# Attention scores as one product per key block, three exponentials per head pair, and tail columns copied by VectorE

## The chip, the cores and the metric

The kernel runs on one core of a Trainium2 chip. The metric is the device time of a run in microseconds; lower is better. The kernel before took 343.55 us in the median of three runs (343.11 to 345.07).

## What is computed

Causal attention with a decay ("forgetting attention"), and behind it a two-layer network with SiLU. There are 8 batches, 8 heads, 576 positions of 64 values; the network is 512 to 2048 to 512 wide over 4608 tokens.

```python
scores = scale * np.matmul(q, k.transpose(0, 1, 3, 2))
cum = np.cumsum(np.log(np.clip(f, 0.0001, 1.0)), axis=-1)
decay = cum[:, :, :, None] - cum[:, :, None, :]
scores = np.where(causal, -1000000000.0, scores + decay)
attn = softmax(scores)                    # written out in the reference
x = np.matmul(attn, v)                    # heads side by side: 4608 x 512
h = x @ w_in
out = (h * (1.0 / (1.0 + np.exp(-h)))) @ w_out
```

The decay is folded into the values: row j of v, and a column of ones beside it, is multiplied by exp(-cum[j]) up to a factor that the division by the sum takes out again. So the kernel needs the exponential of the plain scores, a 0/1 mask on the diagonal blocks, one product with the weighted values, and a division by the product's last column.

## The kernel before

**Stages.** The first 128 queries of all batches (they see only key block 0) are done early. The other 448 queries of a head, "the rest", are done in 32 units, one for each batch and pair of heads (`scores`, `attend`), and the network's two products (`m1_chunk`, L567, and `m2_part`, L612) are dealt out between them. From about 281 us on only the network's products are left.

**Order.** The order of every engine's instructions is the order in which the program issues them (`manual_schedule`), so each engine works through a queue written out by hand. The loop at L874 runs 16 times; I call one pass a round, and its two units n and n+1. A round has three slots of network work (L886, L892, L898) with score products in front of each: chunks 0 and 1 of n; chunk 2 of n and chunk 0 of n+1; chunks 1 and 2 of n+1. Behind the third slot come `attend(n)` and `attend(n+1)`, then a fourth slot. `fill` decides by a count of matmul columns how many network products a slot gets; it knows nothing of the other engines.

**A unit's scores.** A product takes a key block of 128 keys (its 64 values a head on 64 of the 128 rows of TensorE; the pair's second head uses the other 64) and some query columns. `CHUNKS` (L433) gives three PSUM tiles `sc` of two banks a unit, of which two exist: (key block, first column, last column, place). Columns 0 to 384 are queries 128 to 512, columns 384 to 448 the last 64 queries, "the tail". Before, the tail of each of the five key blocks is a product of its own of 64 columns in chunk 2. That makes 12 products a head and unit, 24 a unit.

**Exponentials and masks.** ScalarE takes the exponential of chunks 0 and 1 with 2 x 512 columns each (L463), of chunk 2 with 2 x 128 columns (L463) and, apart from it, of the tails with 2 x 5 x 64 columns (L467). The first three go into the unit's SBUF tile `u` (four buffers), the last into `ut`, one of four tiles with a strip of zeros between the two heads. VectorE multiplies the three diagonal blocks by the 0/1 triangle `tri` in one instruction (`mask`, L476) and the last 64 keys of the tail by `trit` (`mask_tail`, L482).

**Attend.** `attend` forms 28 products with the weighted values into a PSUM tile `dn` (L506 for the rest, L515 for the tail), then VectorE divides (L523, L524). `AT` says where in `u` a block lies.

**The network.** `m1_chunk` writes a PSUM tile `hp` (L567); ScalarE takes a tanh of it (`th`, L575) and VectorE forms `gt` from both (L576). `hp`, `po`, `dn` and `tx` share four PSUM buffers (tag "big"): a product into a fifth tile waits until an earlier one has been read. The last reader of `hp` is L576.

**The feed.** SP's queue loads q, k and v of later units (L158, L168, L179), GpSimd casts q and k to bf16 (L399, L403, three instructions a unit), SP transposes them by DMA into `qkT` (L427, two units ahead), and GpSimd weights the values (`convert_v`, L413, four instructions a batch, in the third and fourth unit of the batch before). From round 3 on SP also transposes the finished rows of the round before (L538, L542).

Of the kernel before, what the change touches and what calls it, by code (L numbers as in the profile page):

```python
# [8 lines left out]
ACT = mybir.ActivationFunctionType  # L9
ALU = mybir.AluOpType  # L10
FP32 = mybir.dt.float32
BF16 = mybir.dt.bfloat16
P = 128
# [5 lines left out]
def kernel(  # L19
# [10 lines left out]
    nc = tc.nc  # L30
# [7 lines left out]
    SM = 512  # L38
    ST = S - SM
    NM = SM // P  # L40
    NR = NM - 1
    RB = NR * P
    RQ = RB + ST
# [8 lines left out]
    scale = 1.0 / float(D) ** 0.5  # L52
# [24 lines left out]
    tri = const.tile([P, P], BF16, name="tri")  # L77
    trit = const.tile([P, ST], BF16, name="trit")
# [6 lines left out]
    uts = [const.tile([P, NM + 1, 3, ST], BF16, name=f"ut_{i}") for i in range(4)]  # L85
# [63 lines left out]
    def head(p, i):  # L149
        return p // 2 * 4 + 2 * i + p % 2  # L150
# [69 lines left out]
    for i in range(2):  # L220
        for g in range(2):
            nc.vector.tensor_copy(
                out=sel[:, i, :].rearrange("p (u w r) -> p u w r", u=2, w=2)[:, g, :, :],
                in_=ident_bf[:, :].rearrange("p (r u i w) -> p u i w r", u=2, i=2, w=2)[
                    :, g, i, :, :
                ],
            )

    def keep_warm(n):
# [7 lines left out]
        out=f_sb[:, :], in0=f_sb[:, :], scalar1=1e-4, scalar2=1.0, op0=ALU.max, op1=ALU.min  # L237
# [185 lines left out]
    def transposes(n):  # L423
# [5 lines left out]
        )  # L429


    T0 = P
    CHUNKS = [  # L433
        [(1, 0, P, 0), (2, P, 2 * P, P), (3, 2 * P, RB, 2 * P), (1, P, 2 * P, RB)],
        [(0, 0, RB, 0), (1, 2 * P, RB, RB)],
        [(2, 2 * P, RB, 0)] + [(kb, RB, RQ, T0 + kb * ST) for kb in range(NM + 1)],
    ]
    UW = 2 * SM + P

    AT = {(c, c): (c - 1) * P for c in range(1, NM)}  # L440
    AT |= {(c, 0): SM + (c - 1) * P for c in range(1, NM)}
    AT |= {(2, 1): RB, (3, 1): SM + RB, (3, 2): 2 * SM}

    def scores(n, c):
        b, p = divmod(n, NP)
        if c == 0:
            us[n] = upool.tile([P, 2, UW], BF16, name="u", tag="u")
        u, ut = us[n], uts[n % 4]
        t = qkT[n]
        sc = psc.tile([P, 2, SM], FP32, name="sc", tag="sc")  # L450
        for kb, q0, q1, o in CHUNKS[c]:
            for i in range(2):
                r = slice(i * D, (i + 1) * D)
                if kb == 0:
                    kt = kT0[b][r, p, :]
                else:
                    k0 = RB if kb == NM else kb * P + RB
                    kt = t[r, k0 : k0 + P]
                nc.tensor.matmul(  # L459
                    sc[:, i, o : o + q1 - q0], lhsT=kt, rhs=t[r, q0:q1], start=True, stop=True  # L460
                )
        w = SM if c < 2 else T0
        nc.scalar.activation(  # L463
            out=u[:, :, c * SM : c * SM + w], in_=sc[:, :, 0:w], func=ACT.Exp, scale=scale
        )
        if c == 2:
            nc.scalar.activation(  # L467
                out=ut[:, :, 0:3:2, :].rearrange("p k i t -> p i k t"),
                in_=sc[:, :, T0 : T0 + (NM + 1) * ST].rearrange("p i (k t) -> p i k t", t=ST),
                func=ACT.Exp,  # L470
                scale=scale,
            )

    def mask(n):
        x = us[n][:, :, 0:RB].rearrange("p i (a t) -> p i a t", t=P)
        nc.vector.tensor_tensor(  # L476
            out=x, in0=x, in1=tri[:, None, None, :].to_broadcast([P, 2, NR, P]), op=ALU.mult
        )

    def mask_tail(n):  # L480
        x = uts[n % 4][:, NM, 0:3:2, :]
        nc.vector.tensor_tensor(  # L482
            out=x, in0=x, in1=trit[:, None, :].to_broadcast([P, 2, ST]), op=ALU.mult
        )

    NGR = 2 * NR + 1
# [3 lines left out]
    def attend(n):  # L490
        b, p = divmod(n, NP)
        if p % 2 == 0:
            xqs[n // 2] = xqp.tile([P, NGR, 2, D], BF16, name="xr", tag="xr", bufs=3)
        xq = xqs[n // 2]
        u, ut = us.pop(n), uts[n % 4]
        dn = pbig.tile([P, NGR, D + 1], FP32, name="dn", tag="big")

        def vals(kb, i):
            h = head(p, i)
            return v0[b][:, h, :] if kb == 0 else vbf[b][:, kb - 1, h, :]  # L500

        for i in range(2):
            for c in range(1, NM):
                for kb in range(c + 1):
                    o = AT[c, kb]
                    nc.tensor.matmul(  # L506
                        dn[:, i * NR + c - 1, :],
                        lhsT=u[:, i, o : o + P],
                        rhs=vals(kb, i),
                        start=(kb == 0),  # L510
                        stop=(kb == c),
                    )
        for i in range(2):
            for kb in range(NM + 1):
                nc.tensor.matmul(  # L515
                    dn[:, NGR - 1, :],
                    lhsT=ut[:, kb, i : i + 2, :].rearrange("p i t -> p (i t)"),
                    rhs=vals(kb, i),
                    start=(i == 0 and kb == 0),
                    stop=(i == 1 and kb == NM),  # L520
                )
        rec = recp.tile([P, NGR], FP32, name="rec", tag="rec")
        nc.vector.reciprocal(out=rec[:, :], in_=dn[:, :, D])  # L523
        nc.vector.tensor_tensor(  # L524
            out=xq[:, :, p % 2, :],
            in0=dn[:, :, 0:D],
            in1=rec[:, :, None].to_broadcast([P, NGR, D]),
            op=ALU.mult,
        )
# [58 lines left out]
    def store(n):  # L588
        n = max(n, 0)
        for q_, dst, src in stores[:n]:  # L590
            q_.dma_start(out=dst, in_=src)  # L591
        del stores[:n]
# [105 lines left out]
    def fill(us_, least=0, ends=(0, 0)):  # L698

        left = us_ + at["left"]  # L700
        kinds = plan(left)
        kinds += [0] * (least - len(kinds))
        if any(ends) and kinds:
            if 2 not in kinds:
                kinds[0] = 2
            n1, n2 = len(kinds) - kinds.count(2), kinds.count(2)
            e0 = 1 if ends[0] else 0
            e1 = 1 if ends[1] and n2 > e0 else 0
            inner = n2 - e0 - e1
            n = n1 + inner  # L710
            mid = [2 if (x + 1) * inner // n > x * inner // n else 1 for x in range(n)]
            if inner and mid[-1] == 2 and e1 and not e0:
                mid = mid[::-1]
            kinds = [2] * e0 + mid + [2] * e1
        for k in kinds:
            t = step(k)
            if t is None:
                at["left"] = 0.0
                return
            left -= t / 1000  # L720
        at["left"] = left
# [117 lines left out]
    def turn(n):  # L839
        if 0 < n < NU - 2:  # L840
            cast_qk(n + 2)
            transposes(n + 2)

    def prepare(n):

        b, p = divmod(n, NP)
        if n != NP - 1 and n + 4 < NU:
            load_qk(n + 4)
        if b + 1 == B:
            return  # L850
        if p == 0 and b > 0:
            load_tails(b + 1)
        if b == 0 and p >= 2 or b > 0 and p == 1:
            for c in range(NM) if b > 0 else range(2 * (p - 2), 2 * (p - 1)):
                load_v(b + 1, c)
        if n == NP - 1:
            load_qk(n + 4)
        if p >= 2:
            for c in range(2 * (p - 2), 2 * (p - 1)) if b > 0 else range(NM * (p - 2)):
                convert_v(b + 1, c)  # L860
# [4 lines left out]
    def slot(us_, *ends):  # L865
        n = len(stores)
        fill(us_, 0, ends)
        store(n)
        for x in pending:
            x[0] -= 1  # L870
        while pending and pending[0][0] == 0:
            ready.update(pending.pop(0)[1])

    for m in range(NQ):  # L874
        n = 2 * m
        piece = 1.7 if m < 2 else 2.4
        scores(n, 0)
        scores(n, 1)
        turn(n)
        if m > 0:  # L880
            back(m - 1)
            if m % 2 == 0:
                b = m // 2 - 1
                pending.append([2, [REST_OF[b]] + ([TAILS_OF[b][0]] if b == NM - 1 else [])])
        prepare(n)
        slot(piece, 1, 0)  # L886
        mask(n)
        scores(n, 2)
        scores(n + 1, 0)
        turn(n + 1)  # L890
        prepare(n + 1)
        slot(piece, 1, 0)  # L892
        mask_tail(n)
        mask(n + 1)
        scores(n + 1, 1)
        scores(n + 1, 2)
        mask_tail(n + 1)
        slot(piece, 1, 0)  # L898
        attend(n)
        attend(n + 1)  # L900
        slot(min(3.5, max(0.8, behind() - LAG)) if m > 1 else 0.8)
# [38 lines left out]
```

## Time and profile before

| | before |
|---|---|
| median of three runs | 343.55 us |
| span of the profiled execution, first to last instruction | 342.2 us |
| median less span | 1.35 us |
| TensorE busy, matmuls | 334.3 us, 3560 matmuls |
| VectorE busy | 180.5 us, 387 instructions |
| ScalarE busy | 216.8 us, 401 instructions |
| GpSimd busy | 130.0 us, 227 instructions |
| score matmuls of the rest, L459 | 768 |
| granted TensorE clock | 0.999 |

The profiled execution has no time of its own besides its span; what lies around the span is taken as the difference to the median.

The page gives for each engine (PE is TensorE, DVE VectorE, ACT ScalarE, POOL GpSimd, SPq the queue of SP) busy time, share and number of instructions. A line of the groups view has line, engine, operation, output tile <- input tiles, shapes, count, then busy time and mean duration in ns, then the idle time of the engine in front of it and what ended that. A line of the timeline has start, duration, engine, line, operation, tiles, count; in brackets the idle time before it and its releaser. Matmuls are pipelined, so a matmul's duration is its latency, and what it costs is read from the starts.

### The profile page before, as it was taken

Reading aid. Unit: us, or ns where it says so; the run is one execution under the profiler, and the core shown is the slowest. Engines: PE = TensorE matmul, PEld = TensorE weight load, DVE = VectorE, ACT = ScalarE, POOL = GpSimd, SP = SyncE. Lnnn points to the kernel's source line nnn. Section 1 sums busy time; section 2 is a strip of 40 time slices with the busy share of each in tenths; the row PEclk is TensorE's granted clock in tenths of the full one; section 3 lists DMA queues with packets and bytes.
Section 4 is the critical chain, followed back from the end, with each engine's and each line's share of the span. In section 5 each row is a group of like instructions: output and inputs, shape, how many; then the busy total and the mean of one; then the engine's idle time right before and its main releaser. Section 6 shows DMA issues by size and latency. Waiting matters only on the chain.

```text
span 342.2 us, 8881 instructions
## 1 busy us (share of the span) xinstructions
PE 334.3 (98%) x3560; PEld 198.6 (58%) x3560; DVE 180.5 (53%) x387; ACT 216.8 (63%) x401; POOL 130.0 (38%) x227
## 2 busy tenths in 40 slices
PE   7999999999999999999999999999999999999995
PEld 3645655567656556566465666656656565555654
DVE  4665736357647547357445563655746364444330
ACT  5857645877687676857759677595685944454431
POOL 8895317732618307327325422612830000001011
PEclk9999999999999999999999999999999999999999
DMA  8999999999699889999999789989994010001012
GB/s 154 185 184 221 192 192 155 233 207 190 142 172 205 188 177 168 180 210 156 174 188 188 171 156 202 169 170 165 165 186 101 22 42 33 31 32 61 33 53 72
DMA packets 142457, 50.67 MB, mean 148 GB/s; under 512 B 133328, under 2 KB 139728, under 8 KB 142416
## 3 DMA queue, kind: packets, MB, share of 16 engines
q1 hardware_dynamic: 132400, 32.93, 56.7%
q0 software_dynamic: 9856, 17.04, 21.5%
q8 instruction: 28, 0.46, 0.6%
q10 hardware_dynamic: 160, 0.13, 0.1%
q14 instruction: 13, 0.11, 0.1%
HBM read 36.85 MB, written 9.44 MB: 135 GB/s over the span
## 4 chain that ended last, share of the span: by engine, by line
PE 66%; DMA 14%; SPq 9%; POOL 6%; issue 3%; ACT 0%; POOLq 0%
PE po L612 29%; PE hp L567 25%; DMA vf<-in_v_dram 6%; PE sc L459 5%; SPq L158 5%; PE dn L506 4%; DMA w_out_bf<-in_moe_w_out_dram 3%; PE dn L515 2%; SPq L427 2%; DMA qkT<-qkb 2%; POOL qkb L399 1%; DMA qkb<-in_k_dram 1%; SPq L168 1%; SPq L179 1%; DMA qf<-in_q_dram 1%
## 5 line engine op out<-in xcount | busy, mean ns | idle before, releaser
L576 DVE SCALAR_TENSOR_TENSOR gt<-th,hp 128x384 bf16<-128x384 bf16 (+2 forms) x208 | 105.8, 522 | 119.0 <-ACT th L575 115.5
L575 ACT ACTIVATE th<-hp 128x384 bf16<-128x384 f32 (+2 forms) x208 | 95.2, 478 | 84.3 <-PE hp L567 82.0
L612 PE MATMUL po<-w_out_bf,gt 128*128 128x512 bf16 (+1 forms) x592 | 145.3, 374 | 0.0
L567 PE MATMUL hp<-x,w_in_bf 128*128 128x384 bf16 (+2 forms) x704 | 128.1, 321 | 0.2
L567 PEld LDWEIGHTS <-w_in_bf 128*128 128x128 bf16 x832 | 79.9, 98 | 56.5 <-issue 0.7
L463 ACT ACTIVATE u<-sc 128x1024 bf16<-128x1024 f32 (+1 forms) x96 | 75.3, 822 | 9.5 <-PE sc L459 9.5
L612 PEld LDWEIGHTS <-gt 128*128 128x128 bf16 x592 | 53.3, 98 | 47.9 <-issue 2.5
L591 POOL DMA_DIRECT2D out_dram<-osb x38 | 21.0, 552 | 93.7 <-ACT osb L622 66.7
L413 POOL TENSOR_TENSOR vp<-vf,w_bf 128x520 bf16<-128x520 f32 (+1 forms) x32 | 34.4, 1078 | 41.0 <-DMA vf<-in_v_dram 35.1
L622 ACT ACTIVATE osb<-po 128x512 f32<-128x512 f32 (+1 forms) x37 | 22.1, 597 | 18.9 <-PE po L612 18.9
L399 POOL CAST qkb<-qf 128x384 bf16<-128x384 f32 x32 | 16.7, 521 | 41.9 <-DMA qf<-in_q_dram 41.2
L459 PE MATMUL sc<-qkT 64*128 64x128 bf16 (+1 forms) x640 | 26.9, 207 | 0.9 <-DMA qkT<-qkb 0.8
L459 PEld LDWEIGHTS <-qkT 64*128 64x128 bf16 x640 | 18.4, 94 | 12.5 <-issue 10.2
L467 ACT ACTIVATE ut<-sc 128x640 bf16<-128x640 f32 x32 | 23.3, 729 | 0.0
L476 DVE TENSOR_TENSOR u<-u,tri 128x768 bf16<-128x768 bf16 x32 | 22.1, 690 | 1.2 <-ACT u L463 1.2
L399 POOL CAST qkb<-kf 128x384 bf16<-128x384 f32 x32 | 17.7, 554 | 13.0 <-DMA kf<-in_k_dram 12.8
L506 PEld LDWEIGHTS <-u 128*128 128x128 bf16 x576 | 20.8, 98 | 2.5
L506 PE MATMUL dn<-vp,u 128*128 128x65 bf16 x384 | 21.8, 194 | 0.0
L524 DVE TENSOR_TENSOR xr<-dn,rec 128x448 bf16<-128x448 f32 x32 | 20.0, 624 | 1.1
L506 PE MATMUL dn<-v,u 128*128 128x65 bf16 x192 | 19.8, 194 | 0.0
L482 DVE TENSOR_TENSOR ut<-ut,trit 128x128 bf16<-128x128 bf16 x32 | 11.2, 351 | 15.6 <-ACT ut L467 15.6
L567 PE MATMUL hp<-xt,w_in_bf 128*128 128x256 bf16 x128 | 17.7, 273 | 0.0
(68 smaller groups left out, 203.0 us busy)
## 6 DMA issues: line engine op xcount, KB each, us to landing
out_dram<-osb POOLq DMA_DIRECT2D x32, 256.0 KB, 3.3
vf<-in_v_dram SPq DMA_DIRECT2D x26, 256.0 KB, 4.7
qf<-in_q_dram SPq DMA_DIRECT2D x64, 96.0 KB, 2.9
kf<-in_k_dram SPq DMA_DIRECT2D x64, 96.0 KB, 3.1
w_in_bf<-in_moe_w_in_dram POOLq DMA_DIRECT2D x4, 512.0 KB, 6.9
w_out_bf<-in_moe_w_out_dram POOLq DMA_DIRECT2D x4, 512.0 KB, 9.6
vf<-in_v_dram POOLq DMA_DIRECT2D x6, 256.0 KB, 10.3
qkb<-in_q_dram POOLq DMA_DIRECT2D x8, 128.0 KB, 5.1
```

Source lines behind the costliest of these rows:

```text
L399: nc.gpsimd.tensor_copy(out=t2[:, c0 : c0 + NR, :].rearrange("p c x -> p (c x)"), in_=t[:, :, :, :].rearrange("p c h d -> p (c h d)"),)
L413: nc.gpsimd.tensor_tensor(out=vbf[b][r, c, :, :], in0=vst[b][c][r, :, :], in1=w_bf[r, c + 1, b * H : (b + 1) * H, None].to_broadcast([n, H ...
L459: nc.tensor.matmul(sc[:, i, o : o + q1 - q0], lhsT=kt, rhs=t[r, q0:q1], start=True, stop=True)
L463: nc.scalar.activation(out=u[:, :, c * SM : c * SM + w], in_=sc[:, :, 0:w], func=ACT.Exp, scale=scale)
L467: nc.scalar.activation(out=ut[:, :, 0:3:2, :].rearrange("p k i t -> p i k t"), in_=sc[:, :, T0 : T0 + (NM + 1) * ST].rearrange("p i (k t) ...
L476: nc.vector.tensor_tensor(out=x, in0=x, in1=tri[:, None, None, :].to_broadcast([P, 2, NR, P]), op=ALU.mult)
L506: nc.tensor.matmul(dn[:, i * NR + c - 1, :], lhsT=u[:, i, o : o + P], rhs=vals(kb, i), start=(kb == 0), stop=(kb == c),)
L567: nc.tensor.matmul(hp[:, :], lhsT=w_in_bf[:, cc, fc * P : (fc + 1) * P], rhs=xcols(g, cc), start=(cc == 0), stop=(cc == NCC - 1),)
L575: nc.scalar.activation(out=th[:, :], in_=hp[:, :], func=ACT.Tanh, scale=0.5)
L576: nc.vector.scalar_tensor_tensor(out=gt[:, fc, :], in0=th[:, :], scalar=1.0, in1=hp[:, :], op0=ALU.add, op1=ALU.mult,)
L612: nc.tensor.matmul(po[:, :], lhsT=gt[:, fc, tb * P : (tb + 1) * P], rhs=w_out_bf[:, fc, m0:m1], start=(fc == 0), stop=(fc == NFC - 1),)
L622: nc.scalar.activation(out=osb[:, :], in_=po[:, :], func=ACT.Copy, scale=0.5)
```

## The change

The tail is no longer a product of its own: the last 64 queries are columns of the same product as the others. A unit has 5 products a head instead of 12 (two for key blocks 2 and 3 in chunk 0, block 1 and the last 64 keys in chunk 1, block 0 in chunk 2), and the columns are the same, 1472 a head. Each chunk has one exponential, into `u`, which becomes wider (1472 columns a head, 1152 before). Since `attend` wants the tail in `ut`, VectorE now copies it there: the last 64 keys with the mask in one instruction (`mask_tail`, from `u` to `ut`), the other four blocks with two copies a unit (`tails`). The mask of the diagonal blocks becomes two instructions, one for blocks 2 and 3 and one for block 1. In `ut` the strips change places (`UT`). The queues of GpSimd and SP keep their order, and so does TensorE's, the score products apart.

```diff
     CHUNKS = [
-        [(1, 0, P, 0), (2, P, 2 * P, P), (3, 2 * P, RB, 2 * P), (1, P, 2 * P, RB)],
-        [(0, 0, RB, 0), (1, 2 * P, RB, RB)],
-        [(2, 2 * P, RB, 0)] + [(kb, RB, RQ, T0 + kb * ST) for kb in range(NM + 1)],
+        [(2, P, RQ, 0), (3, 2 * P, RQ, RQ - P)],
+        [(1, 0, RQ, 0), (NM, RB, RQ, RQ)],
+        [(0, 0, RQ, 0)],
     ]
...
-        w = SM if c < 2 else T0
+        w = SM if c < 2 else RQ
         nc.scalar.activation(
             out=u[:, :, c * SM : c * SM + w], in_=sc[:, :, 0:w], func=ACT.Exp, scale=scale
         )
-        if c == 2:
-            nc.scalar.activation(
-                out=ut[:, :, 0:3:2, :].rearrange("p k i t -> p i k t"),
-                in_=sc[:, :, T0 : T0 + (NM + 1) * ST].rearrange("p i (k t) -> p i k t", t=ST),
-                func=ACT.Exp,
-                scale=scale,
-            )
...
+    def mask(n, kbs):
+        u = us[n]
+        if len(kbs) == 2:
+            o, step_ = UO[2], UO[3] - UO[2]
+            x = u[:, :, o : o + 2 * step_].rearrange("p i (a t) -> p i a t", t=step_)[:, :, :, 0:P]
+            m_ = tri[:, None, None, :].to_broadcast([P, 2, 2, P])
+        else:
+            x = u[:, :, UO[1] : UO[1] + P]
+            m_ = tri[:, None, :].to_broadcast([P, 2, P])
+        nc.vector.tensor_tensor(out=x, in0=x, in1=m_, op=ALU.mult)
...
     def mask_tail(n):
         nc.vector.tensor_tensor(
-            out=x, in0=x, in1=trit[:, None, :].to_broadcast([P, 2, ST]), op=ALU.mult
+            out=uts[n % 4][:, UT[NM], 0:3:2, :],
+            in0=us[n][:, :, UO[NM] : UO[NM] + ST],
+            in1=trit[:, None, :].to_broadcast([P, 2, ST]),
+            op=ALU.mult,
         )
+
+    def tails(n, kbs):
+        o0, o1 = (UO[kb] + RB - UQ[kb] for kb in kbs)
+        u = us[n]
+        e = o1 - o0
+        a0 = o0 - (e - ST)
+        x = u[:, :, a0 : a0 + 2 * e].rearrange("p i (k t) -> p i k t", t=e)[:, :, :, e - ST : e]
+        x0 = UT[kbs[0]]
+        nc.vector.tensor_copy(
+            out=uts[n % 4][:, x0 : x0 + 2, 0:3:2, :].rearrange("p k i t -> p i k t"), in_=x
+        )
...
         slot(piece, 1, 0)
-        mask(n)
+        mask(n, (2, 3))
+        mask(n, (1,))
+        mask_tail(n)
+        tails(n, (2, 3))
         scores(n, 2)
         scores(n + 1, 0)
         turn(n + 1)
         prepare(n + 1)
         slot(piece, 1, 0)
-        mask_tail(n)
-        mask(n + 1)
+        tails(n, (1, 0))
+        mask(n + 1, (2, 3))
+        tails(n + 1, (2, 3))
         scores(n + 1, 1)
         scores(n + 1, 2)
+        mask(n + 1, (1,))
         mask_tail(n + 1)
+        tails(n + 1, (1, 0))
         slot(piece, 1, 0)
         attend(n)
         attend(n + 1)
```

## The prediction

> **What bounds the kernel now.** I read the table of engines first, then the matmul groups by shape, then the timeline of one round.
>
> ```profile
> PE 334.3 (98%) x3560; PEld 198.6 (58%) x3560; DVE 180.5 (53%) x387; ACT 216.8 (63%) x401; POOL 130.0 (38%) x227
> ```
>
> TensorE has work in flight for 98% of the span. From 111.8 to 280 us it is busy 168.20 of 168.20 us at full clock, so only two things can move the end: matmul time itself, or a new wait of TensorE. In the stage of the rounds the waits view has just two waits of score matmuls, both on the transposed queries (0.4 us at 74.38 and at 111.78). The rows that the change touches, by shape:
>
> ```profile
> L463 ACT ACTIVATE u<-sc 128x1024 bf16<-128x1024 f32 x64 | 64.5, 1035 | 9.5 <-PE sc L459 9.5
> ...
> L467 ACT ACTIVATE ut<-sc 128x640 bf16<-128x640 f32 x32 | 23.3, 729 | 0.0
> L476 DVE TENSOR_TENSOR u<-u,tri 128x768 bf16<-128x768 bf16 x32 | 22.1, 690 | 1.2 <-ACT u L463 1.2
> ...
> L463 ACT ACTIVATE u<-sc 128x256 bf16<-128x256 f32 x32 | 12.7, 396 | 0.0
> L482 DVE TENSOR_TENSOR ut<-ut,trit 128x128 bf16<-128x128 bf16 x32 | 11.2, 351 | 15.6 <-ACT ut L467 15.6
> ```
>
> **TensorE.** Per unit 12 pairs of score matmuls become 5; the columns stay 1472 a head. Here is one group (start, duration, engine, line):
>
> ```profile
> 153.82 0.23 PE L459 MATMUL sc<-qkT 64*128 64x128 bf16 x2
> 153.89 0.19 PE L459 MATMUL sc<-qkT,kT 64*128 64x64 bf16 x2
> 153.92 0.50 PE L459 MATMUL sc<-qkT 64*128 64x64 bf16 x16
> 154.35 0.39 PE L612 MATMUL po<-w_out_bf,gt 128*128 128x512 bf16 x1
> ```
>
> Durations are latencies; starts tell the cost. The two heads of a pair start 3 ns apart and run side by side. A pair of 64 columns costs 29 ns from start to start (64 columns at 2.4 a ns are 26.7), a pair of 128 columns 56 (53.3), one of 384 columns 162 to 175 (160). So a removed pair is worth 2.5 ns and wide ones may cost some of it back: 7 x 2.5 = 17 ns a unit, 0.56 us over 32 units, between 0.1 and 0.7. Going into a group of 64-row matmuls and out of it costs about 98 and 95 ns, whatever the width beside it (64, 128, 384 columns); the 48 groups stay. What is saved before 111.78 goes into the wait there. I take **-0.4 us**.
>
> **ScalarE.** 396 and 729 ns become one instruction of 896 elements: 396 + 640 x (1035 - 396)/768 = 929 ns, 196 ns less a unit, 6.3 us in all. ScalarE is 63% busy and TensorE hardly waits for it (0.28 and 0.18 us near 63 and 66 us, ahead of the wait at 74.38, which swallows them). In a round the third slot's first tanh can come up to 0.4 us earlier, which gives VectorE some room; I count that below.
>
> **VectorE.** Two instructions a unit become five. Undisturbed, L476 takes 0.55 us for 768 elements and L482 0.22 us for 128, so 0.15 us + 0.52 ns an element. The two new masks are 0.42 and 0.28, the tail mask 0.22. A copy of 256 elements between SBUF tiles has no row: 0.22 at least (four elements a cycle; L257, 512 elements, took 0.29) and 0.28 at two a cycle. Together 1.36 us against 0.77, 19 us more over 32 units on an engine that is idle 162 us, mostly waiting for a tanh. By busy time this is hidden. But SBUF-to-SBUF work of VectorE is held by work of GpSimd, and that decides. In the round near 244 us, VectorE and then GpSimd:
>
> ```profile
> 243.81 1.12 DVE L482 TENSOR_TENSOR ut<-ut,trit 128x128 bf16<-128x128 bf16 x1
> 244.85 0.55 DVE L476 TENSOR_TENSOR u<-u,tri 128x768 bf16<-128x768 bf16 x1
> 245.32 1.07 DVE L482 TENSOR_TENSOR ut<-ut,trit 128x128 bf16<-128x128 bf16 x1
> 246.32 0.54 DVE L576 SCALAR_TENSOR_TENSOR gt<-th,hp 128x384 bf16<-128x384 bf16 x1
> ```
>
> ```profile
> 243.80 2.51 POOL L413 TENSOR_TENSOR vp<-vf,w_bf 128x520 bf16<-128x520 f32 x2
> ```
>
> L482 needs 0.22 us and takes 1.12 and 1.07: each time it ends as an L413 (1.05 us) ends. The second L413 in turn waits for L476. They take turns, one for one; L576, which reads PSUM, is never stretched (0.54 to 0.56 us in all 128). So during a run of casts and conversions each held VectorE instruction costs a whole GpSimd instruction. Now the round near 158 us, VectorE and GpSimd:
>
> ```profile
> 157.11 1.02 DVE L576 SCALAR_TENSOR_TENSOR gt<-th,hp 128x384 bf16<-128x384 bf16 x2 [1.64 <-ACT th L575]
> 158.05 0.22 DVE L482 TENSOR_TENSOR ut<-ut,trit 128x128 bf16<-128x128 bf16 x1
> 158.18 0.86 DVE L476 TENSOR_TENSOR u<-u,tri 128x768 bf16<-128x768 bf16 x1
> 159.29 0.23 DVE L482 TENSOR_TENSOR ut<-ut,trit 128x128 bf16<-128x128 bf16 x1 [0.24 <-ACT ut L467]
> 159.67 1.02 DVE L576 SCALAR_TENSOR_TENSOR gt<-th,hp 128x384 bf16<-128x384 bf16 x2 [0.16 <-ACT th L575]
> ```
>
> ```profile
> 155.96 2.15 POOL L413 TENSOR_TENSOR vp<-vf,w_bf 128x520 bf16<-128x520 f32 x2 [4.95 <-DMA vf<-in_v_dram]
> 158.05 0.58 POOL L399 CAST qkb<-qf 128x384 bf16<-128x384 f32 x1
> 158.58 0.83 POOL L399 CAST qkb<-kf 128x384 bf16<-128x384 f32 x1
> 159.36 0.31 POOL L403 CAST qkb<-qktf 128x128 bf16<-128x128 f32 x1
> 159.63 2.18 POOL L413 TENSOR_TENSOR vp<-vf,w_bf 128x520 bf16<-128x520 f32 x2
> ```
>
> Queued behind the masks is the third slot's first gt (159.67 to 160.22). It frees the PSUM buffer that the second unit's dn takes: TensorE starts that dn at 160.28, 0.06 us later. Any delay of this gt is a stall of TensorE.
>
> After the change six instructions stand there: copy, mask of two blocks, copy, mask of one, tail mask, copy. If all six take turns: copy after the L413 that ends at 158.11; cast to 158.68; mask (streams 0.27) to 158.95; cast to 159.45; copy to 159.52; small cast to 159.81; mask to 159.94; L413 to 160.99; tail mask to 161.06; L413 to 162.11; copy to 162.2; gt at 162.3 instead of 159.67. TensorE waits 2.55 us. The same count gives these waits, after the room each gt has now (0.05 to 0.42 us): near 130 us 2.3; 158 us 2.55; 186 us 1.4; 214 us 1.25; 244 us 0.3; 88 us 0.15; 104 us 0.55. Sum 8.5. Done on the present order, the count puts the gt 0 to 0.4 us later than traced; less that, 7.1. The one at 104 us (0.25 left) disappears in the wait at 111.78: 6.85. In the other rounds no run of conversions stands beside these masks, or the gt has over 0.7 us of room. Less 0.6 for the earlier tanh and exponentials: **+6.2 us**. The first mask group of a round (four instructions for one) lies under two exponentials, 2 us of ScalarE: nothing.
>
> Whether the copies take turns is not shown. For it: L730, a copy of 64 elements at 7.88 us, took 0.47 and ended with a GpSimd DMA issue (8.33). Against: L257 ran 0.29 us beside another issue, unstretched. The ends are 0 (copies free: then three held instructions stand in the third group, as now) and 8.5; nearest is L482, the same bytes in the same place, which is held. I take held.
>
> The Trainium skill (page "SBUF — State Buffer", section "Who interferes with whom") says that a Vector copy in a two-port mode and a GpSimd instruction exclude each other for a whole instruction. By that rule the sum is the held one; without it, the free one.
>
> GpSimd loses turns too, at most 0.27 us each, three more a unit, in front of casts that feed transposes; their tiles are issued 2.7 to 12 us ahead of use. Counted at zero up to 1 us.
>
> **Sum.** Span 342.2 - 0.4 + 6.2 = 348.0. The median of the runs shown, 343.55, is 1.35 above the span, so 349.4.
>
> **Rivals.**
> 1. *The copies are not held* (ends not slower). Place: the same third group. Three held instructions as now; the gt is then at 159.7 to 160.1, a stall of 0 to 0.4 us in two or three rounds, +0.6, against -0.4 and -0.6: 343.2. It decides as soon as a copy beside an L413 or a cast lasts under 0.3 us. For: L257; TensorE has no other new wait. Against: L482's rows. Chance 0.28.
> 2. *The runs move apart.* Waits of TensorE shift the loads behind SP's transposes of the last round, so casts fall between the groups and half of the waits go: 346.5. Part of the held case's spread.
> 3. *Fewer, wider matmuls give more than 2.5 ns a pair*, 98 ns at a group's edge included. At most one edge a group, 48 x 0.097 = 4.7 us: 339. Against: the edges don't depend on width. Chance 0.06.
> 4. *Held, and the feed falls behind as well*: 354. Chance 0.06.
>
> Held as forecast, from 345.5 to 353: 0.60. The range goes from the free copies to the held ones with room: 342.6 to 353. About 0.5% (1.7 us) is what a measurement of this kernel can tell from no change: faster 0.07, same 0.30, slower 0.63.
>
> **What would show it.** Steps right: score matmuls 320, L463 96 with one form of 896 elements near 0.93 us; copies stretched to 0.5 to 1.1 us beside casts and L413; first dn of the second unit late by 1 to 2.5 us near 130, 158, 186, 214 us; TensorE idle or waiting on DVE gt. Wrong: copies of 0.2 to 0.3 us everywhere; no new wait of TensorE; ScalarE's saving showing in the end.

## The result and the profile after

The change makes the kernel a little slower: 346.23 us (345.31 to 348.19) against 344.52 us (343.11 to 346.17) in 13 runs each, a ratio of 1.0055 (95% interval 1.0033 to 1.0077). The profiled execution took 345.31 us with a span of 343.5 us, 1.3 us over the span of before.

Line numbers are now those of after: L476 and L479 are the masks, L493 is the copy, L517 and L526 are the products of `attend` for the rest and the tail, L578 is `m1_chunk`, L587 the `gt`, L623 `m2_part`. The table of engines and one line of the waits view of after:

```profile
PE 335.1 (98%) x3112; PEld 191.5 (56%) x3112; DVE 197.3 (57%) x483; ACT 215.5 (63%) x369; POOL 128.5 (37%) x227
```

```profile
PE dn L517 <- DVE gt L587: 1.7, 2, 1.0
```

TensorE has 448 matmuls less, VectorE 96 instructions and 16.8 us more, and TensorE waits for a `gt` in front of a `dn`, for which the waits view of before has no line. The groups by shape that stand for the ones shown of before:

```profile
L463 ACT ACTIVATE u<-sc 128x896 bf16<-128x896 f32 x32 | 29.7, 929 | 0.0
...
L493 DVE COPY ut<-u 128x256 bf16<-128x256 bf16 x64 | 21.3, 337 | 3.5 <-ACT u L463 3.5
...
L476 DVE TENSOR_TENSOR u<-u,tri 128x512 bf16<-128x512 bf16 x32 | 16.5, 517 | 0.3
...
L476 DVE TENSOR_TENSOR u<-u,tri 128x256 bf16<-128x256 bf16 x32 | 12.0, 374 | 5.2 <-ACT u L463 5.2
...
L479 DVE TENSOR_TENSOR ut<-u,trit 128x128 bf16<-128x128 bf16 x32 | 8.0, 249 | 0.0
```

The merged exponential takes 929 ns. The copy's mean of 337 ns hides two kinds: 42 of the 64 take 0.21 to 0.23 us, ten 0.24 to 0.35, twelve 0.49 to 1.10.

The round near 133 us of after, first VectorE, then GpSimd, then TensorE:

```profile
130.29 0.57 DVE L493 COPY ut<-u 128x256 bf16<-128x256 bf16 x1
130.78 0.72 DVE L476 TENSOR_TENSOR u<-u,tri 128x512 bf16<-128x512 bf16 x1
131.42 0.31 DVE L493 COPY ut<-u 128x256 bf16<-128x256 bf16 x1
131.65 1.17 DVE L476 TENSOR_TENSOR u<-u,tri 128x256 bf16<-128x256 bf16 x1
132.74 0.21 DVE L479 TENSOR_TENSOR ut<-u,trit 128x128 bf16<-128x128 bf16 x1
132.87 1.07 DVE L493 COPY ut<-u 128x256 bf16<-128x256 bf16 x1
133.87 0.54 DVE L587 SCALAR_TENSOR_TENSOR gt<-th,hp 128x384 bf16<-128x384 bf16 x1
```

```profile
130.27 0.50 POOL L399 CAST qkb<-qf 128x384 bf16<-128x384 f32 x1
130.72 0.51 POOL L399 CAST qkb<-kf 128x384 bf16<-128x384 f32 x1
131.17 0.48 POOL L403 CAST qkb<-qktf 128x128 bf16<-128x128 f32 x1
131.62 2.24 POOL L413 TENSOR_TENSOR vp<-vf,w_bf 128x520 bf16<-128x520 f32 x2
```

```profile
133.18 0.28 PE L526 MATMUL dn<-vp,ut 128*128 128x65 bf16 x4
134.46 0.19 PE L517 MATMUL dn<-v,u 128*128 128x65 bf16 x1 [0.99 <-DVE gt L587]
```

This is the forecast's mechanism to the letter. The mask of 0.28 us and the copy of 0.22 us take 1.17 and 1.07, each as long as one of the two L413 beside it (the two end near 132.7 and 133.86); the first `gt` of the third slot can start only at 133.87, and the second unit's `dn`, whose buffer it frees, starts at 134.46. The four matmuls before it follow each other at 0.03 us, so it would have started at 133.30.

Measured from start to start like that, the waits for `gt` are 0.88 us (107.58), 1.16 us (134.46) and 0.25 us (161.80), 2.29 in all, and there is none in the eight rounds behind. (The waits view counts less, because it starts at the modelled end of the matmul before.) Against it stand the shorter products. The start of the rounds, after less before: -0.36 us in round 1, 0.00 in round 2, +1.45 in round 6, 1.52 in round 8, 1.28 in the last: from round 8 on after gains 0.034 us a round.

### The profile page after: what moved, and what is told of

It reads as the page before. It is cut to its first block, busy times and chain, and to the rows that moved or that the text cites. A ratio compares the mean times of both kernels' runs of the same rounds, so it can differ in the third digit from the quotient of the medians.

```text
span 343.5 us, 8049 instructions
## 1 busy us (share of the span) xinstructions
PE 335.1 (98%) x3112; PEld 191.5 (56%) x3112; DVE 197.3 (57%) x483; ACT 215.5 (63%) x369; POOL 128.5 (37%) x227
## 4 chain that ended last, share of the span: by engine, by line
PE 86%; DVE 5%; ACT 3%; DMA 2%; issue 1%; POOL 1%
PE po L623 35%; PE hp L578 32%; PE sc L459 6%; PE dn L517 4%; PE tp L285 2%; PE dn L526 2%; DMA qkT<-qkb 2%; DVE gt L587 2%; DVE ut L493 2%; PE wm L232 1%; ACT u L463 1%; ACT th L586 1%; PE sc L300 1%; DVE u L476 1%; PE sc L319 1%
## 5 line engine op out<-in xcount | busy, mean ns | idle before, releaser
L587 DVE SCALAR_TENSOR_TENSOR gt<-th,hp 128x384 bf16<-128x384 bf16 (+2 forms) x208 | 105.6, 522 | 110.0 <-ACT th L586 106.6
L623 PE MATMUL po<-w_out_bf,gt 128*128 128x512 bf16 (+1 forms) x592 | 145.2, 374 | 0.0
L578 PE MATMUL hp<-x,w_in_bf 128*128 128x384 bf16 (+2 forms) x704 | 128.2, 321 | 0.2
L578 PEld LDWEIGHTS <-w_in_bf 128*128 128x128 bf16 x832 | 79.9, 98 | 56.5 <-issue 0.9
L463 ACT ACTIVATE u<-sc 128x1024 bf16<-128x1024 f32 (+1 forms) x96 | 90.1, 997 | 9.5 <-PE sc L459 9.5
L623 PEld LDWEIGHTS <-gt 128*128 128x128 bf16 x592 | 53.3, 98 | 52.2 <-issue 9.3
L413 POOL TENSOR_TENSOR vp<-vf,w_bf 128x520 bf16<-128x520 f32 (+1 forms) x32 | 33.8, 1059 | 36.2 <-DMA vf<-in_v_dram 34.5
L476 DVE TENSOR_TENSOR u<-u,tri 128x512 bf16<-128x512 bf16 x64 | 27.2, 445 | 5.5 <-ACT u L463 5.2
L517 PEld LDWEIGHTS <-u 128*128 128x128 bf16 x576 | 20.9, 97 | 4.6 <-issue 2.1
L493 DVE COPY ut<-u 128x256 bf16<-128x256 bf16 x64 | 21.3, 337 | 3.5 <-ACT u L463 3.5
L459 PE MATMUL sc<-qkT 64*128 64x320 bf16 (+3 forms) x256 | 22.2, 272 | 0.9 <-DMA qkT<-qkb 0.8
L517 PE MATMUL dn<-vp,u 128*128 128x65 bf16 x384 | 21.8, 193 | 0.0
L517 PE MATMUL dn<-v,u 128*128 128x65 bf16 x192 | 19.8, 193 | 1.8 <-DVE gt L587 1.7
L578 PE MATMUL hp<-xt,w_in_bf 128*128 128x256 bf16 x128 | 17.7, 273 | 0.0
L459 PEld LDWEIGHTS <-qkT 64*128 64x128 bf16 x256 | 9.5, 94 | 14.3 <-issue 10.6
L526 PE MATMUL dn<-vp,ut 128*128 128x65 bf16 x256 | 14.1, 194 | 0.0
```

Of the source, the lines that this page charges most:

```text
L413: nc.gpsimd.tensor_tensor(out=vbf[b][r, c, :, :], in0=vst[b][c][r, :, :], in1=w_bf[r, c + 1, b * H : (b + 1) * H, None].to_broadcast([n, H ...
L459: nc.tensor.matmul(sc[:, i, o : o + q1 - q0], lhsT=kt, rhs=t[r, q0:q1], start=True, stop=True)
L463: nc.scalar.activation(out=u[:, :, c * SM : c * SM + w], in_=sc[:, :, 0:w], func=ACT.Exp, scale=scale)
L476: nc.vector.tensor_tensor(out=x, in0=x, in1=m_, op=ALU.mult)
L493: nc.vector.tensor_copy(out=uts[n % 4][:, x0 : x0 + 2, 0:3:2, :].rearrange("p k i t -> p i k t"), in_=x)
L517: nc.tensor.matmul(dn[:, i * NR + c - 1, :], lhsT=u[:, i, o : o + P], rhs=vals(kb, i), start=(kb == 0), stop=(kb == c),)
```

## The experiments

All ratios are to before, on the same chip; in brackets the 95% interval. In the expectations H is the forecast's mechanism (the copies are held by GpSimd, the `gt` comes late, TensorE waits), F a rival (the feed: GpSimd loses turns and delivers the transposed queries late), W another (VectorE's added work and its place in the queue, held or not). P and A came up with the first results, and are explained at e5.

**e1: copies through one port.** The copies become a maximum over an axis of length 1, same data, same place.

```diff
-        nc.vector.tensor_copy(
-            out=uts[n % 4][:, x0 : x0 + 2, 0:3:2, :].rearrange("p k i t -> p i k t"), in_=x
+        nc.vector.tensor_reduce(
+            out=uts[n % 4][:, x0 : x0 + 2, 0:3:2, :].rearrange("p k i t -> p i k t"),
+            in_=x[:, :, :, :, None],
+            op=ALU.max,
+            axis=mybir.AxisListType.X,
         )
```

> The changed kernel, its 64 tail copies done by VectorE as a reduction over an axis of length one in place of a copy; same place, same data, same number. Theory H (copies held by GpSimd): this form is not held, so no instruction on L493 lasts over 0.5 us, though each takes longer alone (0.35 to 0.45 us for 0.22); the waits of TensorE at the second unit's dn (0.88, 1.16 and 0.25 us in the profile after) are gone but for 0.3 us; ratio to before 0.997 to 1.001. Rival W (it is VectorE's added work and its place in the queue, held or not): the waits stay or grow, ratio 1.005 or more. Rival F (the feed: GpSimd, held by VectorE, casts later, and the transposed queries come later): between, with the wait at 73 us (1.06 us) as it is.

Measured 344.56 us, ratio 1.000 [0.9977, 1.0023]. The same round, VectorE and GpSimd of e1 (L590 is the `gt` here):

```profile
130.74 0.41 DVE L493 TENSOR_REDUCE ut<-u 128x256 bf16<-128x256 bf16 x1
131.06 0.28 DVE L476 TENSOR_TENSOR u<-u,tri 128x256 bf16<-128x256 bf16 x1
131.26 0.52 DVE L479 TENSOR_TENSOR ut<-u,trit 128x128 bf16<-128x128 bf16 x1
131.71 0.41 DVE L493 TENSOR_REDUCE ut<-u 128x256 bf16<-128x256 bf16 x1
132.03 1.12 DVE L590 SCALAR_TENSOR_TENSOR gt<-th,hp 128x384 bf16<-128x384 bf16 x2
```

```profile
131.12 0.58 POOL L399 CAST qkb<-kf 128x384 bf16<-128x384 f32 x1
131.66 0.29 POOL L403 CAST qkb<-qktf 128x128 bf16<-128x128 f32 x1
131.91 2.18 POOL L413 TENSOR_TENSOR vp<-vf,w_bf 128x520 bf16<-128x520 f32 x2
```

The copy now takes 0.40 to 0.42 us in all 64 places, beside a cast and beside an L413 (131.91) too; the tail mask is still held (0.52). Undisturbed it is twice as long as the plain copy (VectorE is busy 204.7 us instead of 197.3), and yet the change no longer costs anything. Of the waits for `gt` 0.46, 0.62 and 0.21 us are left, more than the 0.3 us expected; masks are still held beside them. So the held copies are what costs, and not VectorE's busy time. (e1 also frees GpSimd from waiting for the copies. That this is the cost is not what the profile of after shows: the score products that wait for the feed near 74 us start at 74.38 us in before and 74.40 in after, and near 111 us after waits less than before.) The Trainium skill, page "SBUF — State Buffer", section "Who interferes with whom", says that on trn2 a reduction never contends with GpSimd and a copy in a two-port mode does. The durations agree: the reductions of e1 never exceed 0.42 us, and the copies of after reach 1.10. In which mode a copy runs, no trace shows.

**e2: no copies.** The tail's four unmasked blocks stay zero (the tail queries' result is left out); everything else is after.

```diff
-        nc.vector.tensor_copy(
-            out=uts[n % 4][:, x0 : x0 + 2, 0:3:2, :].rearrange("p k i t -> p i k t"), in_=x
-        )
...
-        nc.gpsimd.memset(t[:, :, 1, :], 0.0)
+        nc.gpsimd.memset(t[:, :, :, :], 0.0)
```

> The changed kernel without the two copies a unit; the four unmasked tail blocks of ut stay zero, so the last 64 queries of a head see the last 64 keys only. H: three held instructions in the third group as before the change; no wait at dn over 0.3 us; what is left is the saving of wide products, 0.3 to 0.7 us; ratio 0.996 to 1.000. W: the same. F: if the masks alone cost the feed, ratio over 1.002 with waits at the score products.

Measured 344.41 us, 0.999 [0.9964, 1.0015]; one wait for `gt` of 0.30 us is left, but a score product waits 2.13 us for transposed queries at 111.5. Wider products and one exponential fewer, without any copy, bring no gain that can be measured; in the profiled execution the time went into the wait for the feed near 111 us.

**e3: before, with the mask in two instructions.**

```diff
-        x = us[n][:, :, 0:RB].rearrange("p i (a t) -> p i a t", t=P)
...
+        for a0, a1 in ((0, 2), (2, 3)):
+            x = us[n][:, :, a0 * P : a1 * P].rearrange("p i (a t) -> p i a t", t=P)
+            nc.vector.tensor_tensor(
```

> The kernel before, with the mask of three diagonal blocks as two instructions (two blocks, one block), as the change has it; nothing else. One held instruction more in the third group (four for three). H: one GpSimd instruction more is waited for in the rounds with conversions beside it: 0.3 to 1 us at dn in one to three rounds, 0.5 to 1.5 us in all, ratio 1.001 to 1.004. W: 0.13 us of VectorE in a group that waits for a tanh anyway: ratio 1.000.

Measured 344.72 us, 0.9994 [0.9978, 1.001], with waits for `gt` of 0.15 us at 133.4 and 0.55 us at 160.65. The waits are as expected, but the extra held mask can't be measured in the time; the ratio misses the lower end of what was expected.

**e4: values loaded a unit earlier.** The aim is that GpSimd's conversions come earlier in the round.

```diff
-        if b == 0 and p >= 2 or b > 0 and p == 1:
+        if b == 0 and p >= 2 or b > 0 and p == 0:
```

> The changed kernel with the loads of the next batch's values issued in the first unit of a batch in place of the second (from the second batch on), so that GpSimd's conversions no longer wait for them and run several us ahead of the third group of a round. Copies and masks as in the change. H: from the fourth batch on no copy beside a conversion; the waits at dn near 107, 133 and 161 us shrink to under 0.4 us together; ratio 0.997 to 1.002. W: waits stay, ratio 1.005. F: the loads of values now stand ahead of loads of queries and keys; if the feed decides, waits of score products grow by 0.5 us or more.

Measured 348.85 us, 1.0095 [1.0062, 1.0129]: a miss. The waits for `gt` shrink to 0.31 us as expected, but the earlier value loads (at 94.97 us, for 3.58 us) stand in SP's queue in front of the transposes of the unit that TensorE needs next: these are issued at 99.08 us, in after at 95.43. TensorE in e4:

```profile
99.18 0.36 PE L459 MATMUL sc<-qkT,kT 64*128 64x448 bf16 x2
103.00 0.39 PE L459 MATMUL sc<-qkT 64*128 64x320 bf16 x4 [3.46 <-DMA qkT<-qkb]
```

The feed is so tight here that loading the values earlier costs more than it saves. Its six runs also have a mean granted clock of 0.994 (before 0.999); more on that below.

**e5: after once more, e6: after with 2.56 us of extra work, e7: before with the same.** The open question was why 2.3 us of waits came where 7.1 were counted. I call GpSimd's four conversions (L413) of a round with the casts between them its run. P (phase): GpSimd's conversions keep a timetable of their own, so TensorE's first waits make it late against them, and in later rounds the conversions are over before the third group. A (additive): every round pays by itself, so a delay changes nothing. e6 and e7 add twelve matmuls of 512 columns that nobody reads in front of round 3.

```diff
         piece = 1.7 if m < 2 else 2.4
+        if m == 3:
+            keep_warm(12)
         scores(n, 0)
```

> The changed kernel once more, for a second profile of it. H: waits of TensorE at the second unit's dn again in the rounds near 107 and 133 us, each beside a copy (L493) of 0.9 us or more; where GpSimd's conversions begin over 2 us ahead of the third group, none. Ratio to before 1.003 to 1.008. If the waits sit in other rounds, their place is a matter of GpSimd's phase in that execution.

> The changed kernel with 12 more matmuls of 512 columns (2.56 us of zeros, nobody reads them) ahead of round 3, near 96 us. Theory P (phase: GpSimd's casts and conversions follow the loads, not TensorE, so a late TensorE finds them done): the waits at dn near 107 and 133 us go, the wait for transposed queries near 111 us goes too; the extra work costs little, ratio to before 1.004 to 1.008, about the same as the changed kernel without it. Rival A (the runs of GpSimd are tied to the rounds, waits add up): 2.56 us on top, ratio 1.011 to 1.014.

> The kernel before with the same 12 matmuls ahead of round 3. Both theories: 2.56 us less the wait near 111 us (0.6), ratio 1.005 to 1.008. P: equal to the changed kernel with the extra work, within 0.3%. A: the changed kernel stays 0.5% behind.

Measured: e5 346.60 us, 1.0048 [1.0027, 1.0068]; e6 347.25, 1.0069 [1.0047, 1.0092]; e7 347.01, 1.0061 [1.003, 1.0093]. The line of the waits view in e5, then in e6:

```profile
PE dn L517 <- DVE gt L587: 3.1, 3, 1.2
```

```profile
PE dn L517 <- DVE gt L587: 1.5, 1, 1.5
```

e5 repeats the three waits in rounds 3, 5 and 7 (1.04, 1.11, 1.40 us) and has none later. In e6, which enters round 3 late, only round 3 waits (1.70 us). With the extra work the change costs 0.24 us, without it 1.7: the same delay that shifts before's end by 2.1 us takes most of the change's price away. (The two intervals overlap widely, so that 0.24 is zero within the error; resampling the runs puts the difference of 1.4 us between the two prices at 0.3 to 2.5.) This speaks for P; A's 1.011 to 1.014 did not come.

One thing that P expected did not come either: the wait of round 3 did not go, it grew. In front of it e6 has a copy of 1.75 us, the first line, and GpSimd beside it:

```profile
106.89 1.75 DVE L493 COPY ut<-u 128x256 bf16<-128x256 bf16 x1
```

```profile
106.79 0.51 POOL L399 CAST qkb<-kf 128x384 bf16<-128x384 f32 x1
107.24 0.29 POOL L403 CAST qkb<-qktf 128x128 bf16<-128x128 f32 x1
107.50 2.39 POOL L413 TENSOR_TENSOR vp<-vf,w_bf 128x520 bf16<-128x520 f32 x2
```

The copy ends at 108.64 us, 0.09 behind the first of the two L413 (108.55): it was held through two casts and a conversion in a row. So the two engines do not always take turns one for one, as the prediction read it near 244 us.

The starts speak for P too, but not for P alone. From the start of a round's scores to the first L413 of its run, in rounds 3, 5, 7, 9, 11, 13:

| | r3 | r5 | r7 | r9 | r11 | r13 |
|---|---|---|---|---|---|---|
| before | 7.20 | 5.39 | 5.60 | 4.48 | 4.44 | 4.11 us |
| e7, before + 2.56 us | 4.55 | 3.12 | 5.02 | 2.72 | 2.43 | 2.19 |
| after | 6.98 | 4.76 | 2.68 | 1.41 | 0.93 | -1.01 |
| e5, after again | 7.32 | 5.80 | 4.33 | 1.41 | 1.06 | -0.62 |
| e6, after + 2.56 us | 4.48 | 1.79 | 2.23 | 0.65 | -1.04 | -1.11 |

The third group begins 7 to 8 us into a round and a run lasts some 6 us, so a run that starts before about 2 us is nearly over by then. In before, delaying TensorE by 2.56 us moves the run forward in the round by 1.8 to 2.7 us (by 0.6 in round 7): the rounds of e7 begin 2.8 to 3.1 us later than those of before, their runs only 0.5 to 1.2 us later (2.2 in round 7). So GpSimd follows TensorE only in part. What it waits for is mostly the loads, as two lines of the waits view of after show:

```profile
POOL vp L413 <- DMA vf<-in_v_dram: 34.5, 10, 5.1
POOL qkb L399 <- DMA qf<-in_q_dram: 28.8, 13, 4.8
```

SP's queue, which issues the loads, is not quite free of the rounds: in front of the transposes of finished rows it waits for VectorE, in before 13.5 us in 8 waits:

```profile
SPq L538 <- DVE gt L576: 13.5, 8, 4.9
```

TensorE's lateness is not the whole shift against before. In e5 the runs of rounds 9 and 11 come 3.1 and 3.4 us earlier in the round; 2.8 us of each is the later round, the rest the run itself, which starts earlier. In the profiled execution of after, of 3.1 and 3.5 us only 1.5 and 1.4 are the later round, and 1.6 and 2.1 the earlier run. Some of this comes without any copy: in e3 the run of round 9 starts 2.92 us into the round, in before 4.48. Why runs start earlier was not tried.

The round near 158 us in after, GpSimd and VectorE, to be held against the one in the prediction:

```profile
154.45 1.05 POOL L413 TENSOR_TENSOR vp<-vf,w_bf 128x520 bf16<-128x520 f32 x1 [5.13 <-DMA vf<-in_v_dram]
...
156.66 0.70 POOL L399 CAST qkb<-qf 128x384 bf16<-128x384 f32 x1
157.31 0.56 POOL L399 CAST qkb<-kf 128x384 bf16<-128x384 f32 x1
157.83 0.29 POOL L403 CAST qkb<-qktf 128x128 bf16<-128x128 f32 x1
158.08 2.18 POOL L413 TENSOR_TENSOR vp<-vf,w_bf 128x520 bf16<-128x520 f32 x2
```

```profile
159.39 0.95 DVE L493 COPY ut<-u 128x256 bf16<-128x256 bf16 x1
160.26 0.41 DVE L476 TENSOR_TENSOR u<-u,tri 128x512 bf16<-128x512 bf16 x1
160.60 0.21 DVE L493 COPY ut<-u 128x256 bf16<-128x256 bf16 x1
160.73 0.28 DVE L476 TENSOR_TENSOR u<-u,tri 128x256 bf16<-128x256 bf16 x1
160.94 0.21 DVE L479 TENSOR_TENSOR ut<-u,trit 128x128 bf16<-128x128 bf16 x1
161.07 0.21 DVE L493 COPY ut<-u 128x256 bf16<-128x256 bf16 x1
161.21 1.00 DVE L587 SCALAR_TENSOR_TENSOR gt<-th,hp 128x384 bf16<-128x384 bf16 x2
```

The run starts 1.51 us earlier than in before (155.96) though the round starts 1.41 us later. The same six instructions that were to take turns with it meet only its last L413; one is held, five run at their own speed, and TensorE waits 0.25 us instead of 2.55.

**e8: no copies, tail products from `u`.** The tail's products take their weights from `u`, 64 columns wide, into one half of the rows each; `ut` is gone.

```diff
-                    dn[:, NGR - 1, :],
-                    lhsT=ut[:, UT[kb], i : i + 2, :].rearrange("p i t -> p (i t)"),
+                    dn[i * ST : (i + 1) * ST, NGR - 1, :],
+                    lhsT=u[:, i, o : o + ST],
```

> The changed kernel without ut: the tail products take their weights of 64 columns straight from u, each head into its half of dn's rows, so there are no copies, and the tail mask works in place; the same result. H: VectorE's third group has three held instructions, no wait at dn over 0.3 us, as in the run without copies (0.999). New: 64-column tiles. If the two heads' products run side by side, 5 x 27 ns less a unit, 4 us in all; if going in and out of such a tile costs 0.1 to 0.15 us, 6 to 10 us more. Ratio 0.988 to 1.02, open.

Measured 345.95 us, 1.0039 [1.0008, 1.0071]. A pair of the narrow products takes 29 ns from start to start, as long as one wide product, but going into and out of them takes 0.09 to 0.10 us more each time (near 162.6 and 164.8). Together the two `attend` of a round take 1.86 us where those of after take 1.71 (rounds without a wait): 0.15 us a round, 2.4 us in 16 rounds, more than the 1.0 us that e8 takes over before. So e8 shows what narrow products cost and says little on the copies. In the profiled execution, the slowest of its ten, there are waits of 1.55 and 1.61 us in front of score products (73.6, 112.4) and one of 1.12 us for a `gt` (162.9). The masks are still there and can be held.

**e9: four copies a unit instead of two.**

```diff
-        nc.vector.tensor_copy(
-            out=uts[n % 4][:, x0 : x0 + 2, 0:3:2, :].rearrange("p k i t -> p i k t"), in_=x
-        )
+        for i in range(2):
+            nc.vector.tensor_copy(out=uts[n % 4][:, x0 : x0 + 2, 2 * i, :], in_=x[:, i, :, :])
```

> The changed kernel with each copy split by head: four of 128 elements a unit for two of 256; same data. Nine held instructions in the third group for six. P (each wait of TensorE lets GpSimd run ahead, and the waits end once its conversions are over before the group): more and longer waits at dn in rounds 3 to 7, 3 to 5 us in all, none after round 9; ratio 1.007 to 1.012. A (waits recur in every round with conversions): 7 rounds with 2 us and more, ratio over 1.03.

Measured 347.36 us, 1.0068 [1.0042, 1.0095]. Of twice as many copies 15 take 0.43 us or more (in after 12 take 0.49 or more). They bring one longer wait (2.82 us in round 3, behind a copy of 1.77 us that was held as in e6), one of 0.60 us (163.3), and none after. A's figure of over 1.03 falls; the ratio lies just under P's lower end. Doubling the copies hardly raises the price. That one long wait already puts GpSimd ahead fits this, but was not tested apart, and part of e9's price is the clock (last section).

**e10 to e12: another network product in the third slot.** If the third slot ends with its product of the second layer (`m2_part`) instead of beginning with it, its first `m1_chunk` comes earlier, and the second unit's `dn` stands 0.87 us later behind it; the `gt` behind the masks should have more room. e10 does this in after, e11 in before, e12 in after with the copies of e1.

```diff
         tails(n + 1, (1, 0))
-        slot(piece, 1, 0)
+        slot(piece, 0, 1)
         attend(n)
```

> The changed kernel with the pieces of the third slot in another order: the piece of the second network product comes last in place of first, so the second unit's dn comes about 0.87 us later behind the first hp of the slot. VectorE's instructions stay as they are. H: each wait at dn is shorter by up to 0.87 us: at most 0.6 us in all in the profile; ratio 0.997 to 1.002. If the added time were not in these waits: 1.005 as before.

> The kernel before with the same order in the third slot: it has hardly any wait at dn to lose, ratio 0.998 to 1.001.

> The changed kernel with the reduction in place of the copy and the other order in the third slot: no wait at dn over 0.2 us, only the saving of the wide products left (0.4 to 0.6 us) and the waits for transposed queries before 112 us; ratio 0.996 to 1.000.

Measured 347.23 us, 1.0058 [1.0034, 1.0082]; 345.79, 1.0031 [1.0008, 1.0054]; 347.82, 1.0083 [1.0051, 1.0115]. All three miss. The order costs 0.3% by itself, and the waits aren't removed. In e10 those of rounds 3 and 7 move to the first `dn` (1.78 us, ending at 106.23, and 0.59, ending at 161.86), that of round 5 stays at the second (0.91 us, ending at 134.18), and a product of the first layer waits 0.62 us at 115.4. e12 has three waits for `gt` (1.04, 1.13, 0.59 us) and one of 0.87 us on that product; why it is slower than e11 and e1 together suggest stays open. No version with the full result is faster than before beyond the error; the best form of the change is e1, equal to before.

## Why the prediction was right or wrong

- **TensorE, -0.4 us: right.** From round 8 on the rounds gain 0.034 us each, 17 ns a unit, 2.5 ns a removed pair, as worked out. The price of a group's edges did not change. What was saved early was lost in the wait near 74 us, where the transposed queries came no earlier than before (start at 74.40 us, before 74.38), and not in the one at 111.78.
- **ScalarE: right** in size (929 ns measured and forecast) and in its effect: no gain at the end.
- **The copy alone: right**, at the lower bound (0.21 to 0.23 us). **Whether it is held: right.** Twelve copies of 0.49 to 1.10 us each end 0.08 or 0.09 us behind a GpSimd instruction, and e1, which takes just that away, brings the change to 1.000. The rival "the copies are not held" falls, and so does L257's row as evidence: it ran beside a DMA issue, not beside a cast or a conversion.
- **The place in a round: right.** The first `gt` of the third slot is late and the second unit's `dn` waits, near 107, 134 and 162 us. Of the four rounds named as signs, those near 130 and 158 us wait, those near 186 and 214 don't.
- **"The same count gives these waits" (7.1 us, +6.2 in the sum): this step failed.** It took GpSimd's run where the trace of before has it, in every round, and added the waits up. Measured 2.3 us (e5: 3.6), all in rounds 3, 5 and 7. Rounds 9 to 13, with 2.95 us in the count, pay nothing: there the runs start 3 to 5 us earlier in the round than in before. One cause is the waits themselves: they make TensorE late, and GpSimd, which mostly waits for SP's loads, moves with it only in part. The delay of e6 and e7 tests this. The other is that the runs start earlier by themselves, by 0.2 to 2.0 us in e5 and 1.6 to 3.8 in after; its cause stays open. In round 5 of after the wait is half of the count (1.16 against 2.3): of the six instructions two are held for a whole L413 and two for part of a cast. Round 3 paid more than counted, 0.88 against 0.55 us. The count's rule of one turn each was not exact either (e6). The 0.6 us that were taken off for the earlier tanh could not be measured apart.
- **The feed: right** for the profiled execution of after: near 74 us the transposed queries come as late as in before, and what is left of the wait near 111 us (0.1 us) is less than before (0.6).
- **The sum.** Forecast change of the span +5.8 us, measured +1.3; in the medians +1.7. The rival "the runs move apart" named this outcome with 346.5 us, but for another cause (loads pushed behind transposes, so later; the runs came earlier in the round) and only as a part of the spread. That its number is close is luck. The addition from span to time was short too: profiled executions take 1.8 us more than their span (345.31 against 343.5), not 1.35.

What stays open: in after the run of round 7 starts not only earlier in the round but 1.5 us earlier in absolute time (154.45 against 155.96). SP's queue reached the load of the values earlier (150.75 against 151.12) and issued the four in 3.39 us instead of 4.54; why was not tried. In e5, the same kernel, this run starts at 156.31 us, so an execution alone can move it by 1.9 us.

## What to carry to other kernels

Before adding an instruction in front of a tight hand-over on VectorE, look in the timeline at which GpSimd instructions run beside it: a short SBUF copy there can cost a whole GpSimd instruction, in e6 three, and a slower form that isn't held can be cheaper (0.41 us everywhere beat 0.22 us that sometimes became 1.10). When adding up waits over the rounds of a loop, ask what drives the other party: if it has, even in part, its own timetable, the first waits change the phase, and the later ones must not be read from the old trace. Test it with a plain delay, and take a second profile of the same kernel before reading a cause out of one.

## What the runs showed of the hardware that was not expected

A wait of TensorE can cost more than itself, as one profiled execution shows. The stretches of e9 around its long wait (columns: window, length, then busy time and count of PE, PEld, DVE, ACT, POOL, then the granted clock, DMA share, GB/s):

```profile
107.00:108.00 1.00, 0.00 (x0) 0.00 (x0) 1.00 (x2) 0.00 (x0) 1.00 (x4) 1.00 0.85 233
108.00:109.00 1.00, 0.00 (x0) 0.00 (x0) 1.00 (x2) 0.00 (x0) 0.92 (x2) 0.88 0.79 244
109.00:110.00 1.00, 0.71 (x14) 0.70 (x14) 1.00 (x3) 0.00 (x0) 1.00 (x2) 0.50 3.29 161
110.00:111.00 1.00, 1.00 (x20) 0.94 (x18) 0.91 (x3) 0.00 (x0) 0.87 (x2) 0.50 0.08 20
111.00:112.00 1.00, 1.00 (x4) 0.30 (x2) 0.83 (x2) 0.00 (x0) 0.00 (x0) 0.50 0.36 79
112.00:113.00 1.00, 1.00 (x11) 0.48 (x11) 0.17 (x1) 0.69 (x2) 0.74 (x2) 0.92 1.25 322
```

TensorE waits for 2.66 us, until 109.29. The granted clock falls to 0.50 near 108.76 (a mean of 0.88 in that stretch is half clock in the last 0.24 us), 2.1 us into the wait, and is back at full near 112.16. So 2.87 us of matmuls run at half speed, which costs, as an estimate, 1.4 us more. The eleven runs of e9 have a mean clock of 0.9953, the six of e4 0.9938 (before on the same chips 0.9986 and 0.9990): of a span of 345 us that is an estimated 1.2 and 1.8 us, a good part of the 2.7 and 3.9 us that the two cost. In the profiled execution of e4 a wait of 3.46 us left the clock at 1.00, so it doesn't happen every time. In the profiled execution of after, with waits of 1.2 us at most, it stayed at 1.00.

The Trainium skill (page "TensorE: Matmul & The Clock Gate", Part 1) says that the clock is set by windows of 3.41 us that run freely, and halved after an idle one. The half-clock stretch, 3.4 us from 108.76 to 112.16, agrees in length. But if the clock changes at the end of a window, the one that ended at 108.76 began at 105.35, and TensorE was at work until 106.63; an entirely idle window was then not needed. What counts as idle was not tried.
